# Identity products on TensorE: ahead of all work, and in the planned gaps of the first batch of a cosine attention with a two-layer network behind it

## The chip, the cores and the metric

One Trainium2 chip, one NeuronCore of it. The engines spoken of are TensorE (PE; its weight loads are listed as PEld), VectorE (DVE), ScalarE (ACT), GpSimd (POOL) and SyncE (SP), each with an instruction stream of its own; they wait for each other by semaphores. Data sits in device memory, in the on-chip SBUF, and in PSUM, the 8 banks into which TensorE writes. The metric is the device time of one execution in microseconds (us). The kernel before: 442.39 us, median of 5 runs from 438.69 to 444.72.

## The reference

Eight batches, 12 heads, a sequence of 448, a head dimension of 64. Each row of q and k is divided by its norm, scores are divided by tau = 0.1 and go through a softmax, and the result multiplies v. The heads are put side by side (3584 tokens of 768) and go through two layers with a gate between them:

```python
q_n = q / (np.linalg.norm(q, axis=-1, keepdims=True) + 1e-06)
k_n = k / (np.linalg.norm(k, axis=-1, keepdims=True) + 1e-06)
scores = np.matmul(q_n, k_n.transpose(0, 1, 3, 2)) / tau
scores = scores - np.max(scores, axis=-1, keepdims=True)
attn = np.exp(scores)
attn = attn / (np.sum(attn, axis=-1, keepdims=True) + 1e-09)
x = np.matmul(attn, v).astype(np.float32)     # then heads side by side: 3584 x 768
h = x @ w_in                                   # 768 x 2048
g = h * (1.0 / (1.0 + np.exp(-1.702 * h)))
out = (g @ w_out).astype(np.float32)           # 2048 x 768
```

## The kernel before

The unit of the attention is a duo `y`: four heads of one batch, three duos to a batch (24 in all). A duo has two pair groups `g` (two heads each). For the first batch (duos 0 to 2) the work is also cut into two halves `h` of 224 queries, so that the first layer can begin on one half.

The steps of a duo: `load` brings q and k, `load_v` brings v (SP's queue; half of duo 0's q and k comes over ACT's queue). `square` and `reduce` give the squared norms, `root` and `invert` (first batch) or `norm_a` and `norm_b` (later) the inverse norms, and `scale` multiplies q (`ti` = 0) or k (`ti` = 1) by them. `turn_qk` (line 427) transposes the scaled rows on TensorE by seven products with the identity, and `turned_qk` (438) copies the result out of PSUM. `scores_h` (465, first batch), `scores` (465, later) and `scores_l` (491, the last 64 keys) multiply queries and keys; `exp_h`, `exp` and `exp_l` (500) take the exponential on ACT. `cast_v` (416, 420, 421) puts v in place with a column of ones, `last_keys` (454) the last keys. `attend` (528, 539) multiplies the exponentials with v: per call two groups of one product of 130 columns and six of 65. `normalise` (551, 567) divides by the sum, `turn_h` or `turn_x` (577, 586) transposes, `turned_h` (604) copies. From the third batch on, DMA transposes take the place of TensorE's.

The network: `mm1_h` (651, first batch) or `mm1` (621) is the first layer, `tanh` (631) and `gate_h` (663) or `gate` (638) the gate, `mm2` (676) the second layer, `halve` and `store` the output. `load_w_in` (700) is issued by POOL in eight pieces, `load_w_out` (706) in two.

PSUM: two tiles `sp` of two banks for scores (pool `ps_s`) and four tiles `mm` of one bank (pool `ps_m`) for all else; one of the four, `rs_ps`, holds the inverse norms of the first batch until its scaling is over. A product that takes a tile waits until the readers of the tile's last use are through.

The order of the work is written ahead of time. `Plan.add` takes each step with its engine, a cost in us, a due time, the steps it comes after, and the buffers it takes and frees. `Plan.tune` shifts the due times and picks among engines by two fixed strings. `Plan.order` (102 to 183) plays the plan through with these costs and yields the steps with their planned start `now`; `Plan.emit` (85) then issues each step's instructions in that order, so that each engine's queue has a fixed order. The planned costs are for example 0.45 us for `turn_qk`, 0.23 for `scores_h`, 0.5 for `attend` and 1.134 for `mm1_h`. An instruction waits on the chip for what it really needs; the planned times only set the order.

Some loads are held by others (`HOLD`): w_in waits until v of duo 1 has landed, q and k of duo 4 until the first block of w_in has, those of duo 5 until the second has:

```python
HOLD = {
    **{("w_in", i, j): [("load", "v", 1, 1)] for i in range(2) for j in range(2)},
    **{("w_out", i): [("load", "q", 2 * ND - 1)] for i in range(2)},
    ND: [],
    ND + 1: [("w_in", 0, 0)],
    ND + 2: [("w_in", 1, 0)],
    2 * ND: [("w_out", 1)],
}
```

Before the plan is emitted, POOL writes the identity (`make_identity`, 128 x 128, half precision) and the constant columns; TensorE has no instruction of its own until the first `turn_qk`.

Of the kernel before, what the change touches and what calls it, by code (L numbers as in the profile page):

```python
# [10 lines left out]
FP32 = mybir.dt.float32  # L11
FP16 = mybir.dt.float16
# [12 lines left out]
DMA_ENGINES = 16  # L25
PACKET_US = {256: 0.033, 1024: 0.072, 1536: 0.064, 1792: 0.078, 3072: 0.135, 4096: 0.178}
MOE_FROM, MOE_LAG = 8, 9
STEPS = "#$%&()*+,-./0123456789:;<=>?@ABCDEFGHIJKLMNOPQRSTUVWXYZ[]^_abcdefghijklmnopqrst"
DUES = (
    "LKQtTEKJLtIKrKKQKKK#K?MC[YRQPIKPKKK:LC3KFMKWKXgB/VK7K;eC]KKIKLWAH@@KMEKFKTTKCLKKmFBCKHQK=P>RD4S5TlMK1VkI"  # L30
# [30 lines left out]
class Plan:  # L61
# [6 lines left out]
    def add(self, name, eng, us, due, emit, after=(), takes=(), frees=(), dma=None, rows=128, hold=(), turn=False, alts=()):  # L68
        if alts:
            self.alts[name] = ((eng, us), *alts)  # L70
        after = list(after) + list(hold)
        if turn:
            self.turns.append((due, len(self.turns), name))
        self.ops[name] = (eng, us, due, emit, after, takes, frees, dma, rows, hold)

    def tune(self, dues, engines):

        engines = dict(zip(self.alts, map(int, engines)))
        for n, c in zip(list(self.ops), dues):
            eng, us, due, *more = self.ops[n]  # L80
            if n in engines:
                eng, us = self.alts[n][engines[n]]
            self.ops[n] = (eng, us, due + 0.25 * (STEPS.index(c) - 39), *more)

    def emit(self, link):


        names, done, port = list(self.ops), {}, None
        for _, i, emit in self.order():
            eng, takes, hold = self.ops[names[i]][0], self.ops[names[i]][5], self.ops[names[i]][9]  # L90
            insts = emit(eng) if names[i] in self.alts else emit()
            insts = insts or (None,) if isinstance(insts, tuple) else (insts,)
            done[names[i]] = insts[-1]
            for h in hold:
                link(insts[0], done[h])
            if ("port", 1) in takes:
                if eng == "DVE":
                    port = insts[-1]
                elif port is not None:
                    link(insts[0], port)  # L100

    def order(self):

        for n, (_, _, name) in enumerate(sorted(self.turns)):
            eng, us, due, emit, after, takes, frees, *more = self.ops[name]
            takes, frees = [*takes, (("turn", n), 1)], [*frees, (("turn", n + 1), 1)]
            self.ops[name] = (eng, us, due, emit, after, takes, frees, *more)
            self.free["turn", n + 1] = 0
# [78 lines left out]
def kernel(  # L187
# [10 lines left out]
    nc = tc.nc  # L198

    B, H, S, D = q.shape  # L200
# [3 lines left out]
    C = S // 64  # L204
# [32 lines left out]
    ps_m = psum("ps_m", 4)  # L237
# [4 lines left out]
    ident = const.tile([128, 128], FP16)  # L242
# [179 lines left out]
        )  # L422

    def turn_qk(y, ti):
        ps = ps_m.tile([128, 512], FP32, name="mm").bitcast(FP16)[:, : 2 * S].rearrange("q (c s) -> q c s", c=C)
        for c in range(C):
            nc.tensor.transpose(  # L427
                out=ps[:, c],
                in_=qkss[y][:, ti, c].rearrange("p j d -> p (j d)"),
                identity=ident,  # L430
            )
        tpss[y, ti] = ps
# [19 lines left out]
    def last_keys(y, eng):  # L452
# [2 lines left out]
            for r in (slice(0, 64), slice(64, 128))  # L455
        )

    tpss, sps, avps, xss = [{} for _ in range(4)]
    rs_ps = ps_m.tile([128, 512], FP32, name="mm")[:, : ND * 4 * C].rearrange("p (y t j c) -> p y t j c", y=ND, t=2, j=2)

    def score(sp, y, g, n, q0, qn, at):
        qkT = qkTs[y]
        for j in range(2):
            r = slice(64 * j, 64 * j + 64)
            nc.tensor.matmul(  # L465
                out=sp[:, j, at : at + qn],
                lhsT=qkT[r, g, 1, 128 * n : 128 * (n + 1)],
                rhs=qkT[r, g, 0, q0 : q0 + qn],
                start=True,
                stop=True,  # L470
            )
# [6 lines left out]
    def scores_h(y, g, h):  # L478
        if g < 2:
            sp = sps[y, g, h, "h"] = ps_s.tile([128, 2, 512], FP32, name="sp")  # L480
            for n in range(2):
                score(sp, y, g, n, SH * h, SH, SH * n)
        else:
            sp = sps[y, 2, h, "h"] = ps_s.tile([128, 2, 512], FP32, name="sp")
            for g in range(2):
                score(sp, y, g, 2, SH * h, SH, SH * g)

    def scores_l(y, h=None):
        sp = sps[y, "l", h] = ps_s.tile([128, 2, 512], FP32, name="sp")
        for g in range(2):  # L490
            nc.tensor.matmul(  # L491
                out=sp[:, g, :S] if h is None else sp[:, 0, SH * g : SH * (g + 1)],
                lhsT=kLs[y % NE][:, g],
                rhs=qkTs[y][:, g, 0] if h is None else qkTs[y][:, g, 0, SH * h : SH * (h + 1)],
                start=True,
                stop=True,
            )
# [23 lines left out]

    def attend(x, h, short=False):
        ps = avps[x, h] = ps_m.tile([128, 512], FP32, name="mm")
        e, vt = exps[x // 2 % NE][:, x % 2], vts[x % NV]
        for i in range(2):
            a, m = P * (2 * h + i), P if short and i else 128
            o = ps[:m, 130 * i : 130 * (i + 1)]
            nc.tensor.matmul(  # L528
                out=o,
                lhsT=e[:, (C - 1) * S + a : (C - 1) * S + a + m],  # L530
                rhs=vt[:, 3].rearrange("p j d -> p (j d)"),
                start=True,
                stop=False,
                skip_group_check=True,
            )
            for n in range(3):
                for j in range(2):
                    at = (2 * n + j) * S + a
                    nc.tensor.matmul(  # L539
                        out=o[:, (D + 1) * j : (D + 1) * (j + 1)],  # L540
                        lhsT=e[:, at : at + m],
                        rhs=vt[:, n, j],
                        start=False,
                        stop=n == 2,
                        skip_group_check=True,
                    )
# [99 lines left out]

    def mm1_h(h, m):
        ps = mms[h, m, "h"] = ps_m.tile([128, 512], FP32, name="mm")
        for i in range(2):
            for kk in range(KT1):  # L650
                nc.tensor.matmul(  # L651
                    out=ps[:, i * SH : (i + 1) * SH],
                    lhsT=w_in_sb[:, kk, 128 * (m + i) : 128 * (m + i + 1)],
                    rhs=xTs[0, kk][:, h * SH : (h + 1) * SH],
                    start=(kk == 0),
                    stop=(kk == KT1 - 1),
                )
# [46 lines left out]
    def load_w_out(i):  # L704
# [5 lines left out]
    plan = Plan(  # L710
        dict(qk=NQK, v=3, sq=2, qks=4, vt=NV, qkT=NT, kL=NE, sp=2, mm=3, exp=NE)
        | {("n2", 1): 4, ("n2", 2): 2, ("nrm", 1): 4, ("nrm", 2): 8}
        | dict(xs=2, x=2 * HP, th=3, g=1, ost=2, port=1)
    )
    add = plan.add
    port = dict(takes=[("port", 1)], frees=[("port", 1)])
# [7 lines left out]
    def due_of(y):  # L724
        return 2 * y if y < ND else 4 * y
# [12 lines left out]
    for y in range(NDUO):  # L738
        b, s, grp = y // ND, due_of(y), group_of[y]
# [3 lines left out]
        for ti, nm in ((1, "k"), (0, "q")):  # L743
            pl = on_pool(y, ti)
            n = 0.55 if y == 0 else 1
# [22 lines left out]
        else:  # L768
            if y == grp[0]:
                reds = [("red", ti, z) for z in grp for ti in range(2)]  # L770
                n = len(grp)
# [91 lines left out]
    def moe_due(b):  # L863
        return 2 * HP * (b + 1) + MOE_LAG if b else MOE_FROM
# [51 lines left out]
    total, done = sum(u[1] for u in moe), 0.0  # L916
    for name, us, emit, after, takes, frees, tail in moe:
        b, part = divmod(B * done / total, 1)
        start, end = moe_due(b), moe_due(b + 1)
# [41 lines left out]
        )  # L961

    plan.tune(DUES, ENGINES)
    plan.emit(link)
# [1 line left out]
_INS = ['q', 'k', 'v', 'tau', 'moe_w_in', 'moe_w_out']  # L966
_OUTS = [((3584, 768), 'float32')]
# [30 lines left out]
```

## Time and profile before

| what | value |
|---|---|
| median of 5 runs | 442.39 us (438.69 to 444.72) |
| profiled execution, its own time | 436.95 us |
| span of the profile, first to last instruction | 435.0 us |
| PE busy | 408.2 us (94%), 3614 products |
| DVE, ACT, POOL busy | 286.8, 259.7, 124.6 us |
| PE busy in 7.7 to 29.4 us | 14.11 of 21.70 us |
| PE busy in 29.4 to 44.5 us | 13.20 of 15.10 us |
| PE busy in 44.5 to 96.0 us | 50.88 of 51.50 us |
| PE busy in 143.0 to 430.6 us | 287.60 of 287.60 us |

How such lines are read: a line of a timeline has the start in us from the first instruction, the time from the first start to the last end of the instructions merged into it, the engine (with a q where it is the engine's sequencer that issues a transfer), the source line, the operation, out<-in by the program's names, the shapes, how many, and in brackets how long the engine was idle before and what ended that. The time of a product includes its way through the array, so that products overlap; the time from one start to the next is what one costs. For a DMA issue, the landing is counted from the issue.

### The profile page before, as it was taken

The page shows a single profiled execution, that of the slowest core. Times are in us where ns is not written, and L with a number is a line of the kernel's source. Part 1 is how long each engine was busy: PE and PEld are TensorE (multiplying, and loading weights), DVE is VectorE, ACT ScalarE, POOL GpSimd, SP SyncE. Part 2 cuts the span into 40 slices and gives each one's busy share as a digit, 9 for nine tenths or more (in the row PEclk, how much of TensorE's full clock was granted, in tenths as well). Part 3 has the DMA queues.
Part 4 walks back from the last instruction along what each step waited for, and adds up shares of the span by engine and source line. Part 5 has one row for each costly group of instructions (what it writes and reads, how often), then busy time and mean ns, then how long its engine had stood idle before and what let it go on. Part 6 is the DMA issues. An engine that isn't in the chain of part 4 may idle for free.

```text
span 435.0 us, 9229 instructions
## 1 busy us (share of the span) xinstructions
PE 408.2 (94%) x3614; PEld 244.2 (56%) x3614; DVE 286.8 (66%) x701; ACT 259.7 (60%) x383; POOL 124.6 (29%) x202
## 2 busy tenths in 40 slices
PE   1589999998899999999999999999999999999996
PEld 0367787554465555565455655465555555565563
DVE  6768898889997568966985958787841225414410
ACT  4789887746954678656766566767743444414300
POOL 4584641231433266331351433432220000000000
PEclk9999999999999999999999999999999999999999
DMA  8999798998658897889679888676442323020122
GB/s 267 230 207 249 154 209 205 287 258 172 146 129 208 189 192 212 129 199 237 143 183 205 162 183 181 123 163 93 62 69 51 79 55 77 2 57 16 36 74 72
DMA packets 84682, 64.88 MB, mean 149 GB/s; under 512 B 52768, under 2 KB 79648, under 8 KB 84640
## 3 DMA queue, kind: packets, MB, share of 16 engines
q1 hardware_dynamic: 80448, 57.36, 59.4%
q0 software_dynamic: 3744, 6.29, 8.0%
q8 instruction: 28, 0.46, 0.5%
q10 hardware_dynamic: 448, 0.66, 0.4%
q14 instruction: 14, 0.11, 0.1%
HBM read 47.19 MB, written 11.01 MB: 134 GB/s over the span
## 4 chain that ended last, share of the span: by engine, by line
PE 79%; DVE 8%; DMA 7%; ACT 2%; POOL 2%; issue 2%; SPq 0%; DVEq 0%; ACTq 0%; POOLq 0%
PE mm L676 30%; PE mm L621 26%; PE mm L539 8%; PE sp L465 6%; PE mm L651 4%; PE mm L528 3%; DMA qk<-in_q_dram 2%; PE sp L491 2%; DVE gT L638 2%; DMA v<-in_v_dram 2%; DMA qk<-in_k_dram 1%; DVE qks L404 1%; DMA qkT<-qks 1%; DVE n L313 1%; PE mm L427 1%
## 5 line engine op out<-in xcount | busy, mean ns | idle before, releaser
L500 ACT ACTIVATE exp<-sp 128x896 f16<-128x896 f32 (+1 forms) x171 | 147.1, 903 | 56.1 <-PE sp L465 49.8
L676 PE MATMUL mm<-w_out,gT 128*128 128x384 f16 x896 | 155.8, 326 | 1.1 <-DVE xs L567 1.1
L621 PE MATMUL mm<-xT,w_in 128*128 128x448 f16 x672 | 135.1, 353 | 1.9 <-DVE gT L638 1.5
L676 PEld LDWEIGHTS <-gT 128*128 128x128 f16 x896 | 84.4, 98 | 63.3 <-issue 8.4
L631 ACT ACTIVATE th<-mm 128x448 f16<-128x448 f32 x128 | 69.6, 546 | 64.8 <-PE mm L621 60.4
L621 PEld LDWEIGHTS <-w_in 128*128 128x128 f16 x672 | 63.4, 98 | 64.1 <-issue 8.0
L638 DVE SCALAR_TENSOR_TENSOR gT<-th,mm 128x448 f16<-128x448 f16 x112 | 67.8, 617 | 33.9 <-ACT th L631 30.7
L313 DVE TENSOR_REDUCE n<-sq 128x14 f32<-128x896 f32 (+1 forms) x50 | 51.6, 1043 | 12.0 <-ACT sq L305 9.5
L539 PE MATMUL mm<-vt,exp 128*128 128x65 f16 (+1 forms) x1152 | 56.9, 195 | 0.2 <-ACT exp L500 0.2
L539 PEld LDWEIGHTS <-exp 128*128 128x128 f16 (+1 forms) x1152 | 52.3, 100 | 4.0 <-issue 1.0
L465 PE MATMUL sp<-qkT 64*128 64x448 f16 (+1 forms) x324 | 42.5, 346 | 4.8 <-ACT qkT L438 2.4
L528 PE MATMUL mm<-vt,exp 128*128 128x130 f16 x192 | 43.0, 224 | 1.6 <-DVE xs L567 0.8
L689 DVE TENSOR_SCALAR ost<-mm 128x384 f32<-128x384 f32 x27 | 15.0, 554 | 43.8 <-PE mm L676 43.6
L567 DVE TENSOR_TENSOR xs<-mm,rc 112x256 f16<-112x256 f32 x96 | 40.8, 425 | 3.4
L551 DVE RECIPROCAL rc<-mm 112x4 f32<-112x4 f32 x96 | 17.0, 177 | 36.2 <-PE mm L539 36.0
L404 POOL TENSOR_TENSOR qks<-qk,y 128x384 f16<-128x384 f32 (+1 forms) x36 | 25.8, 743 | 42.5 <-DVE y L372 21.6
L305 ACT ACTIVATE sq<-qk 128x896 f32<-128x896 f32 (+1 forms) x30 | 27.3, 913 | 16.0 <-DMA qk<-in_q_dram 10.9
L416 POOL CAST vt<-v 128x384 f16<-128x384 f32 x27 | 13.7, 508 | 78.7 <-PE mm L539 31.4
L690 ACT ACTIVATE ost<-mm 128x384 f32<-128x384 f32 x29 | 14.2, 489 | 31.6 <-PE mm L676 28.6
L304 POOL TENSOR_TENSOR sq<-qk 128x896 f32<-128x896 f32 (+1 forms) x14 | 23.6, 1689 | 22.6 <-DVE kL L454 6.3
L405 POOL TENSOR_TENSOR qks<-qk,y 128x896 f16<-128x896 f32 x13 | 23.9, 1841 | 17.8 <-DVE vt L421 8.3
L528 PEld LDWEIGHTS <-exp 128*128 128x128 f16 x192 | 19.2, 100 | 11.2 <-issue 7.0
(59 smaller groups left out, 259.0 us busy)
## 6 DMA issues: line engine op xcount, KB each, us to landing
v<-in_v_dram SPq DMA_DIRECT2D x48, 256.0 KB, 5.4
out_dram<-ost SPq DMA_DIRECT2D x54, 192.0 KB, 2.8
qk<-in_k_dram SPq DMA_DIRECT2D x23, 448.0 KB, 5.3
qk<-in_q_dram SPq DMA_DIRECT2D x23, 448.0 KB, 4.0
w_in<-in_moe_w_in_dram POOLq DMA_DIRECT2D x8, 384.0 KB, 15.4
w_out<-in_moe_w_out_dram POOLq DMA_DIRECT2D x2, 1536.0 KB, 13.6
qkT<-qks SPq DMA_TRANSPOSE x36, 4.5
xT<-xs SPq DMA_TRANSPOSE x18, 3.0
```

The lines of the kernel that those rows point to most:

```text
L305: return nc.scalar.activation(out=dst, in_=src, func=AF.Square)
L313: return nc.vector.tensor_reduce(out=n2s[y][:, ti, js], in_=sqs[y, ti][:, js], axis=AX.X, op=ALU.add,)
L404: return tuple(eng.tensor_tensor(out=o, in0=a, in1=b, op=ALU.mult) for o, a, b in places(y))
L465: nc.tensor.matmul(out=sp[:, j, at : at + qn], lhsT=qkT[r, g, 1, 128 * n : 128 * (n + 1)], rhs=qkT[r, g, 0, q0 : q0 + qn], start=True, sto ...
L500: return nc.scalar.activation(out=dst, in_=src, func=AF.Exp, scale=inv_tau, **ekw)
L528: nc.tensor.matmul(out=o, lhsT=e[:, (C - 1) * S + a : (C - 1) * S + a + m], rhs=vt[:, 3].rearrange("p j d -> p (j d)"), start=True, stop=F ...
L539: nc.tensor.matmul(out=o[:, (D + 1) * j : (D + 1) * (j + 1)], lhsT=e[:, at : at + m], rhs=vt[:, n, j], start=False, stop=n == 2, skip_grou ...
L567: return nc.vector.tensor_tensor(out=xs, in0=ps[:, :, :D], in1=r[:, :, None].to_broadcast((P, 4, D)), op=ALU.mult,)
L621: nc.tensor.matmul(out=ps[:, :S], lhsT=w_in_sb[:, kk, 128 * m : 128 * (m + 1)], rhs=xTs[b, kk], start=(kk == 0), stop=(kk == KT1 - 1),)
L631: nc.scalar.activation(out=ths[key], in_=mms[key][:, :S], func=AF.Tanh, scale=0.851)
L638: nc.vector.scalar_tensor_tensor(out=gts[b // 2][:, m, (b % 2) * S : (b % 2 + 1) * S], in0=ths.pop((b, m)), scalar=1.0, in1=mms.pop((b, m) ...
L676: nc.tensor.matmul(out=mms[b2, t, n][:, :NW], lhsT=gts[b2][:, kk, 128 * t : 128 * (t + 1)], rhs=w_out_sb[:, kk, NW * n : NW * (n + 1)], st ...
```

## The change

Before the plan is emitted, TensorE is given 64 products of the identity with itself (128 columns) into an `mm` tile that nobody reads. While the plan is emitted, the planned idle time of TensorE ahead of each of its steps is noted, less 0.2 us, for steps planned to start before 48 us. When `turn_qk`, `scores_h`, `scores_l`, `attend` or `mm1_h` takes its PSUM tile, it first issues that time divided by 0.032 products of the identity with 64 of its own columns, into columns of that tile that the step does not use. A step without such a call leaves its gap unused: the next step overwrites it. The order and the due times are left as they are.

```diff
@@ Plan.emit
-    def emit(self, link):
-        names, done, port = list(self.ops), {}, None
-        for _, i, emit in self.order():
+    def emit(self, link, gap):
+        names, done, port, busy = list(self.ops), {}, None, None
+        for now, i, emit in self.order():
+            us = self.ops[names[i]][1]
+            if self.ops[names[i]][0] == "PE" and us:
+                if busy is not None and now < FILL_TO:
+                    gap(now - busy)
+                busy = now + us
@@
+FILL_TO, WARM_UP, FILL_US = 48, 64, 0.032
+    gaps = []
+
+    def gap(us):
+        gaps[:] = [max(0.0, us - 0.2)]
+
+    def fill(corner, width):
+        n = int(sum(gaps) / FILL_US)
+        gaps.clear()
+        for _ in range(n):
+            nc.tensor.matmul(out=corner, lhsT=ident, rhs=ident[:, :width], start=True, stop=True, skip_group_check=True)
@@ turn_qk
+        fill(ps[:, S:], 64)
@@ scores_h (both branches)
+            fill(sp[:, 1, S:], 64)
@@ scores_l
+        fill(sp[:, 1, S:], 64)
@@ attend
+        fill(ps[:, 264:328], 64)
@@ mm1_h
+        fill(ps[:, S:], 64)
@@ before the plan is emitted
-    plan.emit(link)
+    warm = ps_m.tile([128, 512], FP32, name="mm")
+    for _ in range(WARM_UP):
+        nc.tensor.matmul(out=warm[:, :128], lhsT=ident, rhs=ident, start=True, stop=True)
+    plan.emit(link, gap)
```

More of the change, by code (lines that the diff above doesn't have):

```diff
@@ L424, in turn_qk @@
     def turn_qk(y, ti):
-        ps = ps_m.tile([128, 512], FP32, name="mm").bitcast(FP16)[:, : 2 * S].rearrange("q (c s) -> q c s", c=C)
+        ps = ps_m.tile([128, 512], FP32, name="mm")
+        fill(ps[:, S:], 64)
+        ps = ps.bitcast(FP16)[:, : 2 * S].rearrange("q (c s) -> q c s", c=C)
         for c in range(C):
@@ L489, in scores_l @@
         sp = sps[y, "l", h] = ps_s.tile([128, 2, 512], FP32, name="sp")
+        fill(sp[:, 1, S:], 64)
         for g in range(2):
```

## The prediction

> **What bounds the kernel now.** I read the page's head and its 40 slices first, then TensorE's timeline for 0 to 62 us, then the chain of waits and the other engines' timelines for the same stretch.
>
> ```profile
> span 435.0 us, 9229 instructions
> PE 408.2 (94%) x3614; PEld 244.2 (56%) x3614; DVE 286.8 (66%) x701; ACT 259.7 (60%) x383; POOL 124.6 (29%) x202
> PEclk9999999999999999999999999999999999999999
> ...
> q8 instruction: 28, 0.46, 0.5%
> ```
>
> TensorE (PE) is busy for 94% of the span, and its idle time lies almost all in the first 45 us, where loads and normalisation feed it. From 44.5 to 96 us it has no wait to speak of (50.88 us busy of 51.50 by the windows), and from 143 us to its last product it is never idle. So time won before 44.5 us counts only if it brings the work that starts there forward.
>
> The clock digits say full speed everywhere. The durations say otherwise; TensorE's timeline:
>
> ```profile
> 22.41 0.54 PE L539 MATMUL mm<-vt,exp 128*128 128x65 f16 x6
> 22.75 0.34 PE L528 MATMUL mm<-vt,exp 128*112 128x130 f16 x1
> ...
> 26.16 0.95 PE L427 MATMUL mm<-ident,qks 128*128 128x128 f16 x7
> 26.90 0.58 PE L491 MATMUL sp<-qkT,kL 128*128 128x224 f16 x2
> ...
> 28.29 0.93 PE L427 MATMUL mm<-ident,qks 128*128 128x128 f16 x7 [0.33 <-POOL qks L405]
> ...
> 29.49 0.35 PE L539 MATMUL mm<-vt,exp 128*128 128x65 f16 x6
> 29.68 0.22 PE L528 MATMUL mm<-vt,exp 128*128 128x130 f16 x1
> ```
> ```profile
> 44.51 0.56 PE L427 MATMUL mm<-ident,qks 128*128 128x128 f16 x7 [0.83 <-POOL qks L405]
> 44.91 0.26 PE L577 MATMUL mm<-ident,xs 112*128 112x112 f16 x2
> ```
>
> From start to next start, seven transposes take 26.90 - 26.16 = 0.74 us early (106 ns each) and 44.91 - 44.51 = 0.40 us late (57 ns); six 65-column products take 0.34 us (57 ns) at 22.4 us and 0.19 us (32 ns) at 29.5 us. The array runs at half speed until about 29.4 us and at full speed after. In 7.7 to 29.4 us PE is busy 14.11 us of 21.70: at full speed that would be 7.1 us, so 7.1 us is all that a warm array can free here. Whether any of it reaches the end depends on what the dense part waits for. GpSimd's (POOL) and SyncE's timelines, and the landing of the load of k for duo 4:
>
> ```profile
> 18.34 5.16 POOL L700 DMA_DIRECT2D w_in<-in_moe_w_in_dram  x8 [1.86 <-DMA v<-in_v_dram]
> ...
> 24.61 1.98 POOL L404 TENSOR_TENSOR qks<-qk,rs 128x384 f16<-128x384 f32 x3
> 26.55 1.68 POOL L405 TENSOR_TENSOR qks<-qk,rs 128x896 f16<-128x896 f32 x1
> ...
> 41.12 1.68 POOL L304 TENSOR_TENSOR sq<-qk 128x896 f32<-128x896 f32 x1 [5.83 <-ACT th L631]
> 42.76 1.69 POOL L405 TENSOR_TENSOR qks<-qk,y 128x896 f16<-128x896 f32 x1
> ```
> ```profile
> 31.65 0.37 SPq L271 DMA_DIRECT2D qk<-in_k_dram  x1
> ```
> ```profile
> DMA to landing us min/median/max: 9.3/9.3/9.3
> ```
>
> Two fences stand in PE's order. The transposes of q, duo 2, at 28.29 wait for POOL, which issued w_in from 18.34 (when v landed), cast v and scaled k and q. Those of q, duo 3, at 44.51 wait for POOL's scaling at 42.76, queued behind the square at 41.12. The releaser named there, a tanh, ended earlier; the load of k issued at 31.65 lands at 31.65 + 9.3 = 40.95, and that is the real one. That load in turn is held by w_in's first block, whose second piece was issued at 19.0 and landed 12.4 later, at 31.4. None of this asks for PE.
>
> **The change, part by part.**
>
> *Warm-up.* 64 products of 128 columns, as soon as the identity is there (its last write ends at 1.32 us). At 106 ns they take 6.8 us, to 8.1; warm part-way, less. The first transpose stands at 7.77, six more at 8.23: at most 0.4 us late, and their copy on ACT starts only at 10.21, with over 1 us to spare. Cost 0; without that cover 0.4.
>
> *Fills.* A fill count is (planned gap - 0.2)/0.032, and the gaps come from the planner's list, which the change leaves alone. Following it, I count 210 fills at 15 places: ahead of the transposes of q duo 0: 54; first scores: 30; k duo 1: 3; last-key scores duo 0: 11; q duo 1: 17; scores (duo 1, pair group 0): 24; first attend: 6; scores (0, group 1, half 1): 5; scores (0, group 2, half 1): 32; scores (1, group 1): 15; q duo 2: 1; then 5, 5, 1 and 1. Warm, by the 65-column row, 210 x 0.032 = 6.7 us; cold, x 0.057 = 12.0 us. The first 84 lie in idle stretches of 2.98 and 2.36 us (1.7 and 1.0 us warm, 3.1 and 1.7 cold), so they are hidden. So are the 17 in the 0.66 us gap at 17.8, if warm.
>
> A fill writes the product's own tile, so it waits for that tile. Where the gap is a wait for data, it runs inside the gap; where it is a wait for the tile, it runs after the gap and delays the product. The row for the largest such place:
>
> ```profile
> 25.66 0.56 PE L465 MATMUL sp<-qkT 64*128 64x224 f16 x4 [0.71 <-ACT exp L500]
> ```
>
> 32 fills here cost 32 x 0.032 = 1.0 us after the exponential that frees the tile; the 15 a little later cost 0.5 us. Set against this: warm products end sooner. The exponential for 22.43 comes forward by 0.7 us, but ACT's next square needs a load issued at 10.80 that landed 12.2 later, at 23.0, so some 0.65 us is left by 24.7, and the 1.0 eats it. At the first fence the balance is 0 to 0.4 us late on ACT, 0 on PE, which had 0.33 us idle there.
>
> *After the first fence* seven transposes take 0.40 for 0.74 us, 0.34 us sooner, and 12 fills cost 12 x 0.032 = 0.38: zero. PE is idle for 0.83 us before the second fence in any case. *At the second fence* the sum is 0: the dense part starts at 44.5 us as before. Bounds: if warmth were worth all it can free, -7.1 us; if all fills after the first two places ran cold behind waits, 126 x 0.057 = 7.2 us less the idle time in their way.
>
> *Instructions.* 274 products bring 274 weight loads, so 548 instructions on PE's 7228: 28 x 548 / 7228 = 2.1 more packets of the instruction queue, each 0.5% x 16 x 435 / 28 = 1.24 us of one DMA engine. Between 0 (fifteen other engines carry the loads) and 2.6 us later landings; I take 0, since the packets go ahead of need.
>
> **Sum against the profiled execution:** 436.95 us (span 435.0 and 1.95 around it) + 0 = 437.0 us.
>
> **How that stands to the median.** The five runs shown go from 438.69 to 444.72, median 442.39: the profiled execution beats them all, by 5.4 us at the median. Half speed that lasts longer is one thing that would do it. The profiled switch at 29.4 came while PE had mixed short products and waits. If it comes only with the dense first-layer products, PE does its 7.2 us of work between 29.4 and 37.5 at half speed, 7.2 more; 24 of those products at half speed (2.3 us warm by the timeline) add 2.3; and 1.9 us of idle time before 44.5 goes off: up to 7.6 us, and the slowest run is 444.72 - 436.95 = 7.8 above. Transfers cannot easily give such a spread, as after 44.5 us nothing waits for them much. So I expect every execution to look like the profiled one: the change then gains little on the profile and 5.4 us (1.2%) on the median.
>
> The Trainium skill, in "TensorE: Matmul & The Clock Gate", Part 1, has a free-running window of about 3.4 us, of which one must be busy to lift half speed and one idle to bring it back, and tells its reader that the ramp costs under 1% and is not to be fitted. This trace has 21.7 us of half speed after its first product, not 3.4. By the page's window alone the change would be worth at most 3.4 / 2 = 1.7 us, and the gap of 5.4 would have another cause.
>
> **Rivals.**
> 1. *Nothing happens to the median* (about 442). The 5.4 us are late landings, which move the second fence itself. For: DMA is full to 70 us (share 1.1 in 15 to 45 us), and the fence hangs on three loads in a row. Against: the spread is 1.4%, wide for transfers of fixed size.
> 2. *A part* (439.5): landings come 2.6 us later through instruction packets, or the clock falls back in the stretches of some 1.7 us that stay idle at 10.3 and 13.4 us and is regained a few us before the first fence. 436.95 + 2.6 = 439.5.
> 3. *Slower* (446.5): fills behind tile waits on a cold array. Should the array be cold again from 13 us, the 126 later fills add 7.2 us where PE had 1.9 us idle up to the first fence: 5.3 late; 1.9 us idle up to the second leaves 3.4 to 3.5, and up to 1.7 more for a late switch. If the 5.4 us are not of the clock, that is 442.4 + 3.4 to 5.1, around 446.5. It decides once lateness at the first fence passes 1.9 us.
> The warm-up may also fail outright; it then leaves rival 1 or 3.
>
> **Chances.** Forecast 437.0, own range 436.0 to 438.6: 0.53. Rival 1: 0.25, 2: 0.12, 3: 0.10. One per cent, 4.4 us, is about what a measurement can tell here; the line runs at 438.0, so about three quarters of the forecast's chance are faster by over 1%, with a little from the rest: 0.43. Slower by over 1% (above 446.8) is half of rival 3 and an unlucky rival 1: 0.07. Range: 436.0 to 443.0, which takes in rival 2 and most of rival 1.
>
> **What would show it.** Right: from about 8 us on, seven transposes in 0.40 us and six 65-column products in 0.19; 32 fills between ACT's release and the scores near 25; the transposes of q duo 2 still at about 28.3 and of q duo 3 at about 44.5, each after POOL; a span of 435; timed runs closer together than 6 us. Wrong: 106 ns transposes after 15 us (the clock was not held); the second fence moved (landings matter, or PE was the fence); a median that stays at 442 with a warm array (the spread was never the clock's).

## The result

| | before | after |
|---|---|---|
| median of the timed runs | 440.41 us (436.55 to 444.72, 79 runs) | 443.08 us (438.33 to 446.63, 44 runs) |
| standard deviation of these runs | 1.92 us | 2.02 us |
| profiled execution, its own time | 436.95 us | 440.31 us |
| span of the profile | 435.0 us | 438.4 us |

The ratio after/before is 1.0054, 95% interval 1.0037 to 1.0070: the change makes the kernel slower by 0.54%, some 2.4 us. The forecast was 437.0 us, the range ended at 443.0. Two medians of before are in this document: 442.39 us of five runs, which the prediction had, and 440.41 us of 79 runs, those five among them. The ratios leave out runs that were over 1.5% above the fastest of their kernel, 8 of the 44 here.

### The profile page after: what moved, and what is told of

The parts are those of the page before. It is cut to its first block, busy times and chain, and to the rows that moved or that the text cites. A ratio compares the mean times of both kernels' runs of the same rounds, so it can differ in the third digit from the quotient of the medians.

```text
span 438.4 us, 9777 instructions
## 1 busy us (share of the span) xinstructions
PE 417.2 (95%) x3888; PEld 253.7 (58%) x3888; DVE 289.2 (66%) x701; ACT 259.8 (59%) x383; POOL 124.9 (28%) x202
## 4 chain that ended last, share of the span: by engine, by line
PE 77%; DMA 8%; DVE 8%; ACT 2%; POOL 2%; issue 2%; SPq 1%; POOLq 0%; ACTq 0%; DVEq 0%
PE mm L643 27%; PE mm L699 27%; PE mm L561 7%; DMA qk<-in_q_dram 7%; PE sp L483 6%; PE mm L674 3%; PE mm L550 3%; DVE qks L409 2%; PE sp L512 2%; ACT exp L521 1%; DVE n L318 1%; DMA qk<-in_k_dram 1%; POOL qks L410 1%; PE mm L434 1%; PE sp L474 1%
## 5 line engine op out<-in xcount | busy, mean ns | idle before, releaser
L561 PEld LDWEIGHTS <-exp 128*128 128x128 f16 (+1 forms) x1152 | 51.3, 99 | 7.2 <-issue 2.9
L483 PE MATMUL sp<-qkT 64*128 64x448 f16 (+1 forms) x324 | 41.0, 333 | 2.4 <-ACT qkT L445 1.5
L713 ACT ACTIVATE ost<-mm 128x384 f32<-128x384 f32 x29 | 14.2, 489 | 31.6 <-PE mm L699 28.6
L550 PEld LDWEIGHTS <-exp 128*128 128x128 f16 x192 | 19.0, 99 | 10.4 <-issue 6.5
```

The costliest lines, as they stand in the source:

```text
L483: nc.tensor.matmul(out=sp[:, j, at : at + qn], lhsT=qkT[r, g, 1, 128 * n : 128 * (n + 1)], rhs=qkT[r, g, 0, q0 : q0 + qn], start=True, sto ...
L550: nc.tensor.matmul(out=o, lhsT=e[:, (C - 1) * S + a : (C - 1) * S + a + m], rhs=vt[:, 3].rearrange("p j d -> p (j d)"), start=True, stop=F ...
L561: nc.tensor.matmul(out=o[:, (D + 1) * j : (D + 1) * (j + 1)], lhsT=e[:, at : at + m], rhs=vt[:, n, j], start=False, stop=n == 2, skip_grou ...
```

## The profile after: level at 45 us, slower behind it

The page of the changed kernel, its head, the clock digits and the queue that brings TensorE's (PE's) instructions:

```profile
span 438.4 us, 9777 instructions
PE 417.2 (95%) x3888; PEld 253.7 (58%) x3888; DVE 289.2 (66%) x701; ACT 259.8 (59%) x383; POOL 124.9 (28%) x202
PEclk9999999999999999999999999999999999999999
...
q8 instruction: 30, 0.49, 0.5%
```

The 274 products are there (3888 against 3614), 548 instructions more, and two instruction packets more (30 against 28). TensorE's timeline:

```profile
1.38 6.28 PE L989 MATMUL mm<-ident 128*128 128x128 f16 x64 [1.38 <-POOL ident masks.py:199]
...
8.66 1.74 PE L474 MATMUL mm<-ident 128*128 128x64 f16 x54
11.62 0.56 PE L434 MATMUL mm<-ident,qks 128*128 128x128 f16 x7 [1.22 <-POOL qks L410]
12.02 1.04 PE L474 MATMUL sp<-ident 128*128 128x64 f16 x30
...
23.58 1.09 PE L474 MATMUL sp<-ident 128*128 128x64 f16 x32 [0.81 <-ACT exp L521]
24.60 0.36 PE L483 MATMUL sp<-qkT 64*128 64x224 f16 x4
...
27.10 0.56 PE L434 MATMUL mm<-ident,qks 128*128 128x128 f16 x7
...
41.94 0.23 PE L434 MATMUL mm<-ident,qks 128*128 128x128 f16 x1 [1.24 <-DVE qks L409]
...
44.06 0.55 PE L434 MATMUL mm<-ident,qks 128*128 128x128 f16 x7
...
45.10 1.31 PE L674 MATMUL mm<-xT,w_in 128*128 128x224 f16 x12
```

Seven transposes take 12.02 - 11.62 = 0.40 us already at 11.6 us: the array is at full speed. The first 84 fills lie in stretches that were idle. The 32 fills stand behind the exponential and delay the scores by 24.60 - 23.58 = 1.02 us, for which 1.0 was forecast. The transposes of q, duo 2, come 1.2 us sooner than before (27.10 against 28.29) and no longer wait for POOL; those of q, duo 3, at 44.06 against 44.51; and the first layer at 45.10 against 45.20. At 45 us these two profiles are level, as the prediction's sum had it.

One row was not foreseen: the wait of 1.24 us at 41.94. VectorE's and GpSimd's timelines of the same kernel around it:

```profile
37.68 4.21 DVE L409 TENSOR_TENSOR qks<-qk,y 128x384 f16<-128x384 f32 x3
```
```profile
37.88 1.90 POOL L309 TENSOR_TENSOR sq<-qk 128x896 f32<-128x896 f32 x1 [3.83 <-ACT exp L521]
39.74 2.00 POOL L410 TENSOR_TENSOR qks<-qk,y 128x896 f16<-128x896 f32 x1
```

Here the load of k of duo 4, issued at 27.7 us, landed after 8.1 us, at 35.8 and not at 40.95. So GpSimd's square of it (37.88) ran beside VectorE's scaling of k of duo 3, and the three pieces of that scaling took 4.21 us together. In the profile of before, where the square came later (41.12), they took 1.23 us:

```profile
39.12 1.23 DVE L404 TENSOR_TENSOR qks<-qk,y 128x384 f16<-128x384 f32 x3
```

From 45 us on the changed kernel loses 3.4 us (its last product ends at 434.08, before at 430.66). The waits of TensorE between 45 and 440 us name the largest pieces:

```profile
PE mm L550 <- ACT ost L713: 2.0, 1, 2.0
...
PE mm L561 <- ACT exp L521: 1.3, 2, 0.7
```

The first was 0.61 us before (at 87.84) and is 2.04 us now (at 89.30): 1.4 us. The second did not exist: 1.28 us at 291 to 292 us. The wait near 142 us grew by 0.1 us (0.80 to 0.90); the remaining 0.7 us or so is spread thinly. The chain of waits for the second:

```profile
284.40 5.08 DMA qk<-in_q_dram
...
289.51 0.03 ACT sq L310
289.53 0.83 issue
290.36 1.71 ACT exp L521 x2
...
292.12 0.24 PE mm L561 x2
```

The last load of q, issued at 284.40, lands after 5.08 us. ScalarE's square of it sits in ScalarE's queue ahead of the two exponentials that TensorE's products need. Before, the same load took 3.16 us, and TensorE did not wait there.

## The experiments

Ratios are to runs of before taken beside each kernel, with 95% intervals; these had medians of 440.0 to 440.8 us.

### One part of the change at a time

Only the warm-up (`e1`), only the fills (`e2`: one product is left of the warm-up), the warm-up and the fills up to 14 us, which are all in idle stretches (`e3`), and the change once more (`e4`, unaltered).

```diff
-FILL_TO, WARM_UP, FILL_US = 48, 64, 0.032
+FILL_TO, WARM_UP, FILL_US = 0, 64, 0.032     # e1
+FILL_TO, WARM_UP, FILL_US = 48, 1, 0.032     # e2
+FILL_TO, WARM_UP, FILL_US = 14, 64, 0.032    # e3
```

> Only the 64 warm-up products are kept; no fill is issued. Theory A (fills that wait for the product's own tile delay it: 92 of the 210 stand behind such a wait, 2.9 us at 32 ns each and 5.2 us at 57 ns): with no fills the time is that of before, within 0.3%. Theory B (the array, warm from about 7 us, falls back to half speed in the idle stretches and what is then issued runs at 57 ns a piece): the clock falls back sooner than with fills and the time is that of before, but the mean granted clock falls to about 0.98, since the record then shows some 15 to 20 us of half speed. Theory C (548 more instructions on PE mean more instruction packets, which delay loads): 128 more instructions, a quarter of the 0.54% of the changed kernel, so 0.1 to 0.2% above before. Should it be as slow as the changed kernel (0.5% above before), the warm-up alone is the cause and A falls.

> The fills are kept; of the warm-up one product is left. A: the array starts at half speed, so that the fills cost 57 ns each until it turns; 0.5 to 1.0% above before. B: as A, with the turn to full speed earlier than the 29.4 us of before, since the fills raise activity (15 to 26 us). C: 420 more instructions, about three quarters of 0.54%: 0.4% above before.

> Warm-up and the first 84 fills, at the two places where the product waits for data for over 2 us, and none of the 126 later ones. A: no fill stands behind a wait for a tile, so the time is that of before within 0.3%. B: the array stays warm at least until 15 us; the time is that of before or below it by up to 0.3%. C: 148 products, 296 instructions, about half of 0.54%: 0.3% above before.

> The changed kernel as it is, beside the three others on one chip. All theories: 0.4 to 0.7% above before. B asks that its runs with a low mean granted clock (below 0.99) are slower than those with a high one (above 0.994) by 2 us or more. A asks that even the runs with the highest clock stay 1 to 2 us above the like of before.

| | added instructions | median | ratio |
|---|---|---|---|
| e1 warm-up only | 128 | 442.39 us | 1.0032 (0.9992 to 1.0072) |
| e2 fills only | 422 | 440.99 us | 1.0020 (0.9986 to 1.0054) |
| e3 early fills | 296 | 442.19 us | 1.0032 (0.9997 to 1.0067) |
| e4 the change | 548 | 441.16 us | 1.0026 (0.9993 to 1.0059) |

The four can't be told apart by time, and none shows a gain. That fills behind tile waits are the loss is not borne out: e3 has none of them and is no faster than e2, which has all. But the intervals reach 0.35% to each side, and e3's array was at half speed again from 14.2 to 31.2 us; e11 below, which has all the fills, says more. Nor does the warm-up last by itself: in e1 the array is at full speed from 4.1 us and at half speed again from 10.9, when nothing fills the idle stretch. This table of windows of e1 (window; its length, then busy time of PE, PEld, DVE, ACT and POOL; granted clock; DMA share; GB/s) shows the clock at 0.50:

```profile
5.00:10.50 5.50, 2.14 (x33) 1.66 (x29) 5.35 (x13) 3.53 (x8) 3.03 (x3) 1.00 1.04 353
11.00:27.50 16.50, 12.44 (x107) 8.03 (x108) 11.10 (x28) 13.38 (x20) 11.25 (x21) 0.50 1.12 236
```

### Before and after, run again

The kernel before, unaltered, was profiled twice more (`e5`, `e6`, one execution each), and both kernels were timed against before as controls (`e9` before, `e10` after).

> The kernel before, unchanged, for a second profiled execution. In the first one k of duo 4 landed at 41.0 us, and POOL's square of it came after DVE's scaling of k of duo 3 (1.2 us); in the five profiles of changed kernels it landed at 35.8 to 37.1, the two ran side by side, and the scaling took 4.2 us. If that is a matter of the execution and not of the change, this one shows k of duo 4 landed at 36 to 37, the scaling at about 4 us, the transposes of q of duo 3 at 46 to 47 instead of 44.5, and the wait near 88 us at 2 us or more. If it is the change's work, this profile repeats the first: landing at 41, scaling 1.2, transposes at 44.5, wait 0.6.

> As the second execution of the kernel before; it tells how far such readings repeat from one execution to the next. Expected by the theory that the execution decides: at least one of the two has the scaling at 4 us; by the theory that the change decides: neither.

> The kernel before, unchanged, as one of the compared kernels: its ratio shows what the comparison makes of no change (0.998 to 1.002), and its profile gives the burst on this chip: 16.4 to 17.4 us if the burst is the kernel's, 18 us or more if it is the chip's (the three profiles of before so far came from other chips than those of the experiments).

> The changed kernel, unchanged, beside them: 0.3 to 0.7% above before; burst 17.6 to 18.8 us if it is the kernel's, the same as the control's if it is the chip's.

The two single executions took 438.32 and 439.85 us. e9 came out at 1.0017 (0.9982 to 1.0051), e10 at 1.0073 (1.0043 to 1.0103). A kernel against itself can thus show 0.2%, and the change is slower again. What counts more is in the profiles: all three new ones of before show the slow scaling. VectorE's timeline of e6:

```profile
38.69 4.21 DVE L404 TENSOR_TENSOR qks<-qk,y 128x384 f16<-128x384 f32 x3
```

So that is not the change's doing. The profiled execution that the prediction read was the unusual one: its k of duo 4 landed at 41.0 us, in the three others of before at 35.9 to 36.3 and in those of the change at 35.8, 35.9 and 40.3. The transposes of q, duo 2, start at 27.30, 27.05 and 26.90 us in e5, e6 and e9, so the 27.10 of the changed kernel is no gain; those of q, duo 3, at 44.42, 45.62 and 45.71. The first layer starts at 45.43, 46.91 and 46.63 us there, and at 45.46 and 44.55 in the profiles of e4 and e10: set against all four profiles of before, the changed kernel's head is about 1 us sooner, not level. The loads between the landing of w_out and that of q of duo 8 took 16.40, 17.36, 16.51 and 19.22 us in the four profiles of before, and 17.61, 18.39 and 17.44 in those of after. The wait near 88 us moves with this burst (0.61, 1.61, 0.84 and 3.56 us in before). The first of the two losses, 0.61 to 2.04 us, is therefore within what before does by itself. The second is not: TensorE waits after the last load of q in each of the three profiles of after (1.28, 0.57 and 1.85 us) and in none of the four of before.

### The number of instructions

The profile's queue q8 brought 28 packets of 0.46 MB / 28 = 16 KB before and 30 after, for 7228 and 7776 instructions of TensorE (products and weight loads): one packet for some 258 or 259, which fits 256. If so, a packet's place in time is set by how many instructions have gone before it. Adding 548 = 2 x 256 + 36 then moves every later packet 36 instructions ahead. Two runs add instructions without warmth and with it: 64 products of one column ahead of all work (`e7`, 128 instructions, 1.87 us of TensorE), and 16 products of 512 columns (`e8`, 32 instructions).

```diff
+    thin = ps_m.tile([128, 512], FP32, name="mm")
+    for _ in range(64):
+        nc.tensor.matmul(out=thin[:, :1], lhsT=ident, rhs=ident[:, :1], start=True, stop=True)
     plan.emit(link)
```
```diff
+    wide = ps_m.tile([128, 512], FP32, name="mm")
+    four = bass.AP(ident.tensor, ident.offset, [ident.ap[0], (0, 4), ident.ap[1]])
+    for _ in range(16):
+        nc.tensor.matmul(out=wide, lhsT=ident, rhs=four, start=True, stop=True)
     plan.emit(link)
```

> The kernel before with 64 products of the identity with one of its columns ahead of the plan: as many instructions as the warm-up, but hardly any column to stream. Theory C (longer instruction stream, other places in memory): as slow as the warm-up alone, +0.3% and a burst of loads after w_out (from w_out's landing to that of q of duo 8) of 18 us or more. Theory W (what costs is the early warm-up, its full speed and the fall back from it): as the kernel before, within 0.2%, the burst as in the control; PE's first transposes at 106 ns and the clock first up near 28 to 31 us.

> The kernel before with a warm-up of 16 products of 512 columns (the identity four times over): as long on the array as the 64 of 128 columns, with 32 instructions in place of 128. Theory W: as slow as the warm-up alone, +0.3%, with the clock up at 4 to 8 us. Theory C: as the kernel before, within 0.1%.

e7: 441.38 us, 1.0027 (0.9995 to 1.0059). e8: 443.36 us, 1.0054 (1.0017 to 1.0092), with a quarter of e7's instructions; their number as such hardly explains it, though the intervals overlap. (In e8 the clock fell to half speed again from 10.4 to 30.9 us, so its warmth did not last either.) The remainder of 256 became the suspect. Three runs test it: the change with 46 products of warm-up in place of 64, which makes 512 added instructions (`e11`); before with 18 one-column products, 36 instructions, no warmth, no fill (`e12`); before with 128 of them, 256 instructions (`e16`).

```diff
-FILL_TO, WARM_UP, FILL_US = 48, 64, 0.032
+FILL_TO, WARM_UP, FILL_US = 48, 46, 0.032    # e11
-    for _ in range(64):                           # as in e7
+    for _ in range(18):                           # e12
+    for _ in range(128):                          # e16
```

> The changed kernel with a warm-up of 46 products in place of 64, so that 512 instructions are added instead of 548: two whole packets of 256, remainder 0 as in the kernel before. Theory P (the place of PE's instruction packets against the loads): the packet comes 2.5 to 3 us after the last q load's issue, the load lands after 3.2 to 3.5 us, no wait of PE near 290 us, and the time is about 1.2 us nearer to before than the changed kernel's (ratio 1.001 to 1.004). Theory W (the warm array itself): the load and the ratio stay as in the changed kernel (1.005 to 1.007).

> The kernel before with 18 products of one column ahead of the plan: 36 instructions, the remainder that 548 leaves, and no warmth. Theory P: the packet comes about 1.0 us after the last q load's issue, the load lands after 4.2 to 5.7 us, PE waits 0.5 to 1.9 us near 290 us, ratio 1.002 to 1.005. Theory W: landing after 3.2 to 3.5 us, no wait there, ratio 1.000 within 0.002.

> The kernel before with 128 products of one column ahead of the plan: 256 instructions, one whole packet. Theory P (the remainder decides): ratio 1.000 within 0.002, the packet 2.5 to 3 us after the last q load's issue, landing after 3.2 to 3.5 us, no wait near 290 us. Rival (each added instruction costs): more than the 18 thin products, 1.006 or above.

e11: 440.38 us, 1.0007 (0.9979 to 1.0036). e12: 442.77 us, 1.0064 (1.0036 to 1.0092). Eighteen tiny products that do nothing cost what the whole change costs, and the whole change with 18 products fewer costs nothing that shows. The last load of q in e11, and in e12 (its issue, and from issue to landing), and TensorE's timeline of e12 behind it:

```profile
L276 SPq DMA_DIRECT2D qk<-in_q_dram x1: 368/368/368, 287.7 to 287.7; - x1
...
DMA to landing us min/median/max: 3.5/3.5/3.5
```
```profile
L271 SPq DMA_DIRECT2D qk<-in_q_dram x1: 373/373/373, 287.8 to 287.8; - x1
...
DMA to landing us min/median/max: 5.6/5.6/5.6
```
```profile
295.17 0.24 PE L539 MATMUL mm<-vt,exp 128*128 128x65 f16 x2 [1.19 <-ACT exp L500]
295.98 0.24 PE L539 MATMUL mm<-vt,exp 128*128 128x65 f16 x2 [0.57 <-ACT exp L500]
```

Issued at the same moment, the load lands 2.1 us later in e12, and TensorE waits 1.76 us that e11 doesn't have. The trace's record of each packet gives the rest, for every kernel of this study (e8's profiled execution was the slowest of its twelve):

| added instructions, remainder of 256 | kernels | packet starts after the load's issue | load lands after | TensorE waits behind it |
|---|---|---|---|---|
| 0 | before, e5, e6, e9, e11, e13, e14, e15, e18 | 2.4 to 3.0 us | 3.2 to 3.5 us | none |
| 0 | e16 | 3.1 us | 3.9 us | 0.29 us |
| 32 to 40 | after, e3, e4, e8, e10, e12, e17 | 0.4 to 1.1 us | 4.2 to 5.7 us | 0.5 to 1.9 us |
| 128 | e1, e7 | 4.1 to 4.2 us before it, the next 7.6 after | 3.4 to 3.5 us | none |
| 166 | e2 | 7.4 us | 3.5 us | none |

In the changed kernel the packet falls into the load's first two microseconds. The DMA view from 285.4 to 286.6 us:

```profile
q8 instruction: 1, 0.02, 8.5%
```

8.5% of 16 engines over 1.2 us are 1.6 us of one engine's time, by the packet's own record 1.64. In the profile of before it took 0.93 us, in the load's tail. The record doesn't name the engines, but it has the load itself, as 256 pieces of 1792 bytes. Before, the last piece ended 2.72 us after the issue. In the changed kernel 241 pieces had ended by 2.95 us, and the other 15 ended one behind the other, the last at 4.48 us; a sixteenth of 256 is 16. In the seven profiles with a remainder of 32 to 40, 8 to 15 pieces end after 2.95 us; in e16 3 do, in the other twelve none. So what comes late is about one engine's share of the load; that it is the engine with the packet is concluded from the times alone.

The Trainium skill, "Runtime: NRT & Kernel Launch", section "Instruction fetch mechanics", has the same unit, blocks of 16 KiB or 256 instructions that the sequencer fetches ahead over a DMA queue of its own, at a cost that is "mostly hidden". These runs agree with the unit, and in the changed kernel's waits from 45 us on TensorE waits only for other engines' results. They differ for the loads beside it: 0.8 to 2.3 us on a load (4.2 to 5.7 against some 3.4), 0.5 to 1.9 us of waits of TensorE.

e16 came out at 441.89 us, 1.0031 (1.0000 to 1.0062), between what the two accounts expected. Its last load behaves (0.29 us of wait), and its 128 products end at 5.0 us, before TensorE has work. Its clock fell back to half speed for 28.2 to 31.7 and 45.3 to 48.7 us; the second of these is in e11 too (44.2 to 47.6). Whether that is its 0.3%, or whether there is any, is open. With e7 (1.0027) it leaves room for some price of added instructions as such, against which e11 speaks, with 512 of them at 1.0007.

### Taking away the collision of GpSimd and VectorE

The slow scaling is in both kernels, in most executions. One added dependency starts GpSimd's square of k, duo 4, only when VectorE's scaling of k, duo 3, is over. It was run in the kernel before (`e13`, again `e15`), in the change with 46 products (`e14`, again `e18`), and in the change as it is (`e17`).

```diff
@@ Plan.emit, before a step's instructions are linked to their holders
+            if names[i] == ("sq", 1, 4):
+                link(insts[0], done["scale", 1, 3])
```

> The kernel before, with POOL's square of k of duo 4 made to wait until DVE has scaled k of duo 3. Theory S (the two slow each other when side by side: three pieces of DVE's scaling take 0.56, 2.04 and 1.77 us in place of 0.56, 0.55 and 0.28): the scaling takes 1.2 to 1.4 us, PE loses its wait of 1.24 us near 42 us, the transposes of q of duo 3 come 1 to 2 us earlier, and the time is 0.2 to 0.5% below before. Rival: the scaling's length comes from its operand, or the square's delay is handed on to POOL's scaling of q and from there to PE: 4 us as before, or no gain at 45 us, ratio 1.000 within 0.002.

> The kernel of the held square once more: 0.3 to 0.6% below before, DVE's scaling at 1.2 to 1.4 us.

> The change with whole packets (46 warm-up products) and POOL's square held until DVE's scaling is through. If the early warm array is worth something once the collision no longer sets the start of the dense part: below e15 by 0.1 to 0.4%. If the head is still set by loads, DVE and POOL: level with e15 within 0.15% (ratio 0.995 to 0.998).

> The change as it is (64 warm-up products, remainder 36) with POOL's square held. If the remainder costs what it cost so far and adds to the rest: 0.4 to 0.6% above e18, ratio 0.995 to 0.998, the packet about 1.0 us after the last q load's issue, a wait of PE near 285 us. If it was the warm-up that cost: level with e18 only if the 18 further products cost nothing, and no such wait.

> Whole packets, warm array and held square once more: ratio 0.990 to 0.995, no wait of PE near 285 us, transposes of q of duo 3 at 41.5 to 42.5 us.

VectorE's timeline, then GpSimd's, of e13:

```profile
39.43 1.23 DVE L406 TENSOR_TENSOR qks<-qk,y 128x384 f16<-128x384 f32 x3
```
```profile
40.90 1.68 POOL L306 TENSOR_TENSOR sq<-qk 128x896 f32<-128x896 f32 x1 [6.11 <-DVE qks L406]
```

The scaling is back at 1.23 us and the square at 1.68, one after the other.

| | median | ratio | transposes of q, duo 3 | w_out landed |
|---|---|---|---|---|
| e13 held square | 438.18 us | 0.9957 (0.9931 to 0.9982) | 44.28 us | 70.27 us |
| e15 held square, again | 437.49 us | 0.9939 (0.9907 to 0.9971) | 43.42 us | 69.22 us |
| e14 held square, change with 46 | 435.91 us | 0.9914 (0.9883 to 0.9945) | 41.62 us | 68.45 us |
| e18 held square, change with 46, again | 437.68 us | 0.9930 (0.9895 to 0.9966) | 42.26 us | 67.92 us |
| e17 held square, change with 64 | 440.32 us | 0.9984 (0.9946 to 1.0021) | 41.75 us | 67.74 us |

(e14 has 7 timed runs, the others 12.) Held, the square is worth about 0.5% without any warmth. e17 and e18 were timed beside each other and differ by 18 identity products alone: e17 is 2.6 us slower. TensorE's waits from 200 us on are one row in e17 and none in e18:

```profile
PE mm L563 <- ACT exp L523: 1.5, 2, 1.0
```

It is the wait behind the last load of q, which lands after 5.3 us in e17 and after 3.5 in e18. Both e14 and e18 beat both kernels. Whether the warm array adds to the held square is not settled by time: the intervals of e14 and e18 overlap those of e13 and e15. At the head, the transposes of q, duo 3, come 1.2 to 2.7 us sooner in the profiles of e14, e17 and e18 than in those of e13 and e15, and in e18 the burst of loads behind w_out (19.95 us) took it back. But that is not shown to be warmth: e18's array was at half speed until 14.2 us (seven transposes take 13.08 - 12.35 = 0.73 us there), and e11, which was warm from 6.6 us but for the windows from 16.9 to 20.3 and from 44.2 us on, has the same transposes at 46.93 us, later than any profile of before.

## Why the prediction was wrong

From the forecast of 437.0 to the 443.08 us measured it is 6.1 us. Of these, 3.4 are the distance from the profiled execution to the median of before (440.41), which the change was to remove and did not; 2.7 are what it made worse (2.4 by the ratio). Two steps failed: the spread put down to the clock, and the 0 for the instruction packets.

*The head: right part by part, its sum by luck.* Warm-up hidden, 84 fills hidden, 32 fills behind their tile wait at 1.02 us for 1.0 forecast, the array warm from 6.7 us on in the changed kernel. Both profiles are level at 45 us (45.10 against 45.20), but the one of before was the earliest there of four (the others 45.43 to 46.91). The first fence did not hold as read: the transposes of q, duo 2, came at 27.10 without a wait for POOL (as they do in e5 and e9 of before), where "about 28.3" was expected. Rival 3's price, fills on a cold array behind waits, fell due for one window at most (16.5 to 19.9 us in e10).

*"The second fence": right sum, wrong cause.* I took the late landing of k, duo 4, for the kernel's habit. It was that one execution's. Usually it lands some microseconds earlier, and the fence is VectorE's scaling running beside GpSimd's square. Whether the fence, with that removed, asks for TensorE, against "None of this asks for PE", is not settled (41.62 to 42.26 us in e14, e17 and e18 against 43.42 and 44.28, with the reserve made above).

*"I take 0, since the packets go ahead of need": the term that made the kernel slower.* I counted 2.1 more packets at 1.24 us and asked only whether two more would delay loads. What acts is the place of all packets behind the added instructions: 36 instructions beyond whole packets move one from the tail of the last load of q to its start, and the load is not over before its last sixteenth has landed, whatever the fifteen other engines do. It measured 0.57 to 1.85 us of TensorE's time in the profiles of the change, against 0 taken and 2.6 at the bound; e11 and e12 show that it goes with the remainder, and comes without any warmth. The full 2.4 us of the ratio are more than the 1.2 us that the wait has on average in the three profiles; e12, at 2.8 us (1.6 to 4.1), has a like excess over its 1.76. What else the moved packets meet was not found. More lapses of the clock are one candidate for the changed kernel: of its timed runs in the ratio, the 9 at a mean granted clock of 0.990 or less have a mean of 443.4 us, the 12 at 0.995 to 0.998 one of 441.7. In e12 it is hardly that: its seven runs at 0.995 to 0.998 have a mean of 443.2 us, those of before at the same clock 439.8.

*"So I expect every execution to look like the profiled one": failed, and with it the 5.4 us.* With the array warm in every profile of the change from 4.5 to 6.7 us on, but for one lapse of 3.4 us in two of them, the timed runs spread as before: standard deviations 2.02 and 1.92 us. So the spread is not that of the first clock switch, which in the four profiles of before came at 28.2 to 30.6 us. The loads' landings move from execution to execution (the burst: 16.4 to 19.2 us in one kernel), and the clock falls back behind some waits, in both kernels. In e6, after the wait of 1.24 us at 42.95, for one window:

```profile
44.40:47.60 3.20, 3.20 (x35) 2.68 (x30) 3.12 (x8) 2.28 (x4) 0.03 (x1) 0.50 1.01 200
```

The timed runs of before in these experiments, grouped by their mean granted clock, show it too: at 0.999 or more the mean was 438.7 us (18 runs); at 0.995 to 0.998, 439.8 (74); at 0.991 to 0.994, 441.4 (52). The 5.4 us were also in part luck of a sample: against 79 runs they are 3.5. Rival 1, for which "the 5.4 us are late landings", was the nearest in its number, though not in its detail: the fast execution that was profiled is the one in which k of duo 4 landed late. With the moved packet on top the median left the range by 0.1 us.

The Trainium skill's rule in "TensorE: Matmul & The Clock Gate", Part 1, that the ramp costs under 1% and that no particular count of slow products should be fitted, was a better guide than my reading of the spread: e14 and e18 differ from e13 and e15 by 0.1 to 0.4%, with overlapping intervals, and no run here shows a warm head to be worth more.

## What to carry to other kernels

Instructions added to TensorE moved every later instruction packet of it here; where one falls into a load that an engine is about to wait for, the price stands hundreds of microseconds away from the edit. So compare kernels by the remainder of 256 too, and try an edit padded or trimmed to whole packets before it is judged. Look at several executions before a fence is read out of one: here the profiled one was the exception, and its distance to the median was no cost of any single cause. A change whose gain ends in a wait of other engines is best tried together with that wait removed.

## What was not expected of the hardware

- VectorE and GpSimd slow each other when both multiply float32 tensors out of SBUF: the three pieces of the scaling took 0.56, 2.03 and 1.77 us beside GpSimd's square and scaling, against 1.23 us in all alone; GpSimd's square took 1.90 us against 1.68 (in e7, where it began later, 1.69), its scaling 2.00 against 1.69. The Trainium skill, "GPSIMD Engine Reference", section 1, names the contention (VectorE instructions with two SBUF inputs) without a price; these rows give one.
- An instruction packet of 16 KB took 0.9 to 2.3 us of DMA time, and where it started within 1.1 us of the issue of a load of 448 KB, that load landed 0.8 to 2.3 us later.
- The granted clock fell to 0.50 for single windows of 3.4 us in dense work, behind or within waits of TensorE of 1.23 to 2.97 us in nearly all cases (the exception: 0.80 and 0.24 us in e16), and not with each such wait (not with the 1.24 us at 41.9 and the 2.04 us at 89 us in the changed kernel).
- The clock digits of the page say full speed from the start until the first switch is recorded, whatever the array does: e2's first record is at 14.5 us, that of before at 29.4, and the durations showed half speed until then.
